# Another order for batch 0's attention and for batch 1's mixing in a fused sorted-attention and mixer kernel

## The chip, the cores and the metric

The kernel runs on one core of a Trainium2 chip. The metric is the device time of one execution in microseconds; unless a unit is given, numbers below are microseconds. The engines are TensorE (PE; its weight loads are listed as PEld), VectorE (DVE), ScalarE (ACT), GpSimd (POOL) and SyncE (SP). Here GpSimd issues all loads that change the type on the way, and SyncE issues the stores, the bounce through DRAM and the DMA transposes. Each engine takes its instructions strictly in order.

## The reference

Four batches, 8 heads, 768 rows of 64. The keys and values come in 8 blocks of 96 rows, and a small 8 x 8 matrix per head, normalized five times, mixes whole blocks. Attention is then block by block, and its output goes through a mixer with a token product and two channel products:

```python
for _ in range(5):
    P = P - np.max(P, axis=-1, keepdims=True)
    P = np.exp(P)
    P = P / (np.sum(P, axis=-1, keepdims=True) + 1e-09)
    P = P / (np.sum(P, axis=-2, keepdims=True) + 1e-09)
k_sorted = np.einsum('bhij,bhjcd->bhicd', P, k_b)
v_sorted = np.einsum('bhij,bhjcd->bhicd', P, v_b)
...   # softmax(q_b k_sorted^T / 8) v_sorted within each block, heads joined to x: 4 x 768 x 512
a1 = alpha1 * x + beta1
tok = np.einsum('ts,bsd->btd', w_tok, a1)
u = x + lam * tok
a2 = alpha2 * u + beta2
ch = np.maximum(a2 @ w_ch1, 0.0) @ w_ch2
return (u + lam * ch)
```

## The kernel before

**Stages.** Until about 12 the block matrix is normalized, on VectorE and ScalarE, while the first loads arrive. From 12 to 37 batch 0's attention runs. From then on the channel products of the mixer run, the largest part of the work, and the attention of the following batch is put in between them piece by piece. A batch has three groups g of 256 tokens. A group has eight steps `h` 0 to 7 (`h_unit`: eight matmuls with `W1p` into `h_ps`, then ReLU to `hT` on ScalarE) and then seven steps `c` (`ch_step`: products with `W2p` and with sums of it, in a scheme with seven half products, with `hs` as sums of `hT`); batch 0's group 0 has eight plain steps `c` instead (`ch_plain`).

**Where the order is set.** All of it is written out by hand. The table `at` holds, under a key (batch, group, h or c, step), what is issued right behind that step; `put` enters it and `run` issues it. What stands earlier in the program stands earlier in each engine's queue. An engine that waits holds up all that is queued behind it.

**Attention of batch 0.** `v_sort` copies columns of v into `VD` so that `v_mix` can mix the blocks on TensorE, 8 columns at a time, with a 512-wide filler matmul ahead; the result is copied to `Vs`. `k_turn` mixes and turns the keys of a pair of heads, and `k_copy` brings them to `KT0` in two parts. `score(b, g, hf)` computes scores for pair g and half hf of the blocks, and ScalarE takes the exponential into `et`. `pv_first` multiplies by `Vs` and VectorE divides by the sums into `x`. `permute` reorders the columns of `w_tok` into `wp`, `prep_wtok` transposes them. `first_mm`, `first_turn`, `first_finish` make the first group's channel input directly (`tok`, `z`, `a2T`); `first_back` makes its `u` and reads the row `brow`.

**Attention of the other batches.** `mix_v` (three pieces) mixes v on TensorE into `mixed`, `bounce_v` writes it to a DRAM scratch (`vscr`), `back_v` reads it back into `Vs` with the rows in the place wanted. `mix_k` (three pieces, four copies to `kT` each) makes the keys, `q_turn_late` or DMA transposes (`q_cross`) the queries. Then come eight scores and eight products `pv`, s0 to s7 and p0 to p7; p_n needs s_n's exponential and `Vs`. `half_done` (tails, `token_affine`) turns half of x into the token product's input `a`; `moe_tok` is the token product, `moe_cross` turns u by DMA transpose into `uT`, `moe_affine` scales it to `a2T`, which the steps `h` of its group read. `weights` prepares the sums of `W2p` on VectorE.

**Buffers and queues around the change.** There are two PSUM pools: `psA`, two buffers of two banks, used in turn by k_turn, scores, pv, mix_v and mix_k; and `psB`, four buffers of one bank. The third tile from a pool of two waits until the first has been read. `uT` and `brow`/`rrow` share two buffers, `raw` (the next batch's v and k) shares two with batch 0's k and v, and `wp` shares one with the first q. Each DMA that GpSimd issues carries one of eight semaphores in turn and waits for the DMA eight before it. GpSimd's queue is, in order: q, v, k, four loads of w_tok, alphaB, betaB, three v_sort copies, lamB, four loads of `W1p` (lines 179 and 180), `brow` (a product of betaB and lamB), four loads of `W2p` (line 317), `lift` (three operations on lamB, alphaB, betaB), then batch 1's v, k and q.

The lines that enter batch 1's work, as the kernel before has them:

```python
for n, at_ in enumerate((("h", 7), ("c", 0), ("c", 1))):
    put(0, 0, *at_, lambda n=n: mix_v(1, n, dve.tensor_copy))
put(0, 0, "c", 1, lambda: bounce_v(1))
put(0, 0, "c", 6, lambda: back_v(1))
seq = ("s0", "s1", "s2", "p0", "s3", "p1", "p2", "s4", "p3", "s5", "p4", "s6", "p5", "s7", "p6", "p7")
slots = [(1, "h", n) for n in range(1, 8)] + [(1, "c", n) for n in range(7)] + [(2, "h", n) for n in range(2)]
```

Of the kernel before, what the change touches and what calls it, by code (L numbers as in the profile page):

```python
# [16 lines left out]
def kernel(  # L17
# [156 lines left out]
    lamB = const([128, C], FT, "lamB")  # L174
    pool.dma_start(alphaB[:], moe_alpha1.partition_broadcast(128))
    pool.dma_start(betaB[:], moe_beta1.partition_broadcast(128))
    for lo, hi in ((8, 16), (16, 32), (32, 48)):
        v_sort(lo, hi, pool.tensor_copy)
    pool.dma_start(lamB[:], moe_lam.partition_broadcast(128))
    for g in range(4):  # L180
        pool.dma_start(W1p[:, :, g * 512:(g + 1) * 512], w1v[:, :, g * 512:(g + 1) * 512])
    brow = att.tile([128, C], F16, name="brow", tag="uT", bufs=2)
    rrow = att.tile([128, GS], F16, name="rrow", tag="uT", bufs=2)
    pool.tensor_tensor(brow[:], betaB[:], lamB[:], ALU.mult)

    vscr = dram.tile([B, H * NB, BLK, D], F16, name="vscr", tag="vscr")
# [50 lines left out]
    def turn_slab(src, rhs, g, name, ps):  # L237
        if ps is psa:
            ps = ps([128, 2, 512], FT, name)
            ps = [ps[:, a, 0:384] for a in range(2)]  # L240
        else:
            ps = [ps([128, 384], FT, name)[:] for a in range(2)]
        for s in range(12):
            for h2 in range(2):
                t = (s + 6 * h2) % 12
                r = slice(h2 * 64, h2 * 64 + 64)
                pe.matmul(
                    ps[t // 6][r, (t % 6) * 64:(t % 6) * 64 + 64],
                    src[r, g, t * D:(t + 1) * D], rhs(r, g), start=True, stop=True,
                )  # L250
        return ps
# [63 lines left out]

    for g in range(4):
        pool.dma_start(W2p[:, g * 4:(g + 1) * 4, :], w2v[:, g * 4:(g + 1) * 4, :])

    bigK = {}
# [68 lines left out]
    def k_copy(b, g, ps, half, eng):  # L388
        eng(
            KT0[:, g, :, :].rearrange("p i (th u) -> p (i th) u", th=2)[:, :, 0:HB].rearrange(  # L390
                "p x (c t) -> p x c t", t=12
            )[:, :, :, half * 6:half * 6 + 6],
            ps[half].rearrange("p (t x c) -> p x c t", t=6, c=4),
        )

# [464 lines left out]
    def wtok(ks, eng):  # L860
        prep_wtok(ks, 0, psb, eng)

    mix_values(0, psb)
    mix_keys(0, psb)
    warm(3)
    v_mix(0, 0, psb, act.copy)
    v_mix(0, 1, psb, act.copy)
    v_sort(48, 56, act.copy)
    v_mix(0, 2, psb, copy)
# [4 lines left out]
    v_mix(0, 3, psb, copy)  # L874
    v_sort(56, 64, act.copy)
    kp2 = k_turn(0, 2, psb)
    k_copy(0, 1, kp1, 0, copy)
    k_copy(0, 1, kp1, 1, act.copy)
    score(0, 0, 0, psa)
    kp3 = k_turn(0, 3, psb)  # L880
    k_copy(0, 2, kp2, 0, copy)
    k_copy(0, 2, kp2, 1, copy)
    score(0, 0, 1, psa)
    v_mix(0, 4, psb, copy)
    k_copy(0, 3, kp3, 0, copy)
    k_copy(0, 3, kp3, 1, copy)
    score(0, 1, 0, psa)
    v_mix(0, 5, psb, copy)
    score(0, 1, 1, psa)
    prep_scales()  # L890
    dve.tensor_copy(Vs[:, :, D:GRP], mgap[:].unsqueeze(2).to_broadcast([128, H * NB, GRP - D]))
    v_mix(0, 6, psb, copy)
    score(0, 2, 0, psa)
    v_mix(0, 7, psb, copy)
    score(0, 2, 1, psa)
    permute(0, copy, 0, 6)
    pv_first(0)
    score(0, 3, 0, psa)
    pv_first(1)
    for ks in range(3):  # L900
        wtok(ks, act.copy)
    score(0, 3, 1, psa)
    wtok(3, act.copy)
    wtok(4, copy)
    wtok(5, copy)
    permute(1, copy, 0, 6)
    first_mm(0, psb)
    row_sums(psb)
    pv_first(2)
    first_turn(0, psb)  # L910
    first_mm(1, psb)
    pv_first(3)
    first_turn(1, psb)
# [30 lines left out]
    put(0, 0, "c", 5, lambda: moe_affine(0, 1))  # L944
    put(0, 1, "h", 3, lambda: moe_affine(0, 2))
    for n, at_ in enumerate(((0, "c", 4), (0, "c", 6), (0, "c", 7), (1, "h", 0))):
        put(0, *at_, lambda n=n: weights(n))
# [10 lines left out]

    for n, at_ in enumerate((("h", 7), ("c", 0), ("c", 1))):
        put(0, 0, *at_, lambda n=n: mix_v(1, n, dve.tensor_copy))  # L960
    put(0, 0, "c", 1, lambda: bounce_v(1))
    put(0, 0, "c", 6, lambda: back_v(1))
    for n, at_ in enumerate((("c", 2), ("c", 4), ("c", 6))):
        put(0, 0, *at_, lambda n=n: mix_k(1, n, (act.copy,) * 4))
    for g, at_ in enumerate(((0, "c", 5), (0, "c", 6), (0, "c", 7), (1, "h", 0))):
        put(0, *at_, lambda g=g: q_turn_late(1, g, act.copy))
    put(0, 1, "h", 6, lambda: load_kv(2), lambda: load_q(2))
    seq = ("s0", "s1", "s2", "p0", "s3", "p1", "p2", "s4", "p3", "s5", "p4", "s6", "p5", "s7", "p6", "p7")
    slots = [(1, "h", n) for n in range(1, 8)] + [(1, "c", n) for n in range(7)] + [(2, "h", n) for n in range(2)]
    for what, at_ in zip(seq, slots):  # L970
        put(0, *at_, attn(1, what[0], int(what[1])))
    put(0, 1, "c", 3, half_done(1, 0))

    for b in range(1, B):
        p = b - 1
        if b > 1:
            for n, at_ in enumerate(((2, "h", 3), (2, "h", 5), (2, "h", 7)) if b == 2 else ((2, "h", 1), (2, "h", 3), (2, "h", 5))):
                put(p - 1, *at_, lambda b=b, n=n: mix_v(b, n, act.copy))
            put(p - 1, 2, "h", 7, lambda b=b: bounce_v(b))
            put(p - 1, 2, "c", 6, lambda b=b: back_v(b))  # L980
            for n in range(3):
                at_ = ((p - 1, 2, "c", 4), (p - 1, 2, "c", 6), (p, 0, "h", 1)) if b == 2 else (
                    (p - 1, 1, "c", 6), (p - 1, 2, "c", 4), (p - 1, 2, "c", 6)
                )
                put(*at_[n], lambda b=b, n=n: mix_k(b, n, (act.copy,) * 4))
            for kt in range(NT):
                put(p - 1, *((2, "h", 0) if b == 2 else (1, "c", 1)), lambda b=b, kt=kt: q_cross(b, kt))
            if b + 1 < B:
                put(p, 0, "c", 0, lambda b=b: load_kv(b + 1), lambda b=b: load_q(b + 1))
            for what, at_ in (  # L990
                ("s0", (0, "h", 5)), ("s2", (0, "c", 1)), ("p0", (0, "c", 3)), ("s4", (0, "c", 5)), ("p2", (1, "h", 1)),
                ("s6", (1, "h", 3)), ("p4", (1, "c", 1)), ("p6", (1, "c", 4)),
            ):
                for i in range(2):
                    put(p, *at_, attn(b, what[0], int(what[1]) + i))
            put(p, 1, "h", 2, half_done(b, 0))
        put(p, 2, "h", 2 if b == 1 else 0, half_done(b, 1))
        put(p, 2, "h", 6 if b == 1 else 5, lambda b=b: moe_tok(b, 0, psb))
        put(p, 2, "h", 7 if b == 1 else 6, lambda b=b: moe_tok(b, 1, psb), lambda b=b: moe_cross(b, 0))
        put(p, 2, "c", 5 if b == 1 else 4, lambda b=b: moe_affine(b, 0))  # L1000
        put(b, 0, "h", 0, lambda b=b: moe_tok(b, 2, psb))
# [59 lines left out]
```

The softmax here doesn't subtract the row's maximum and nothing guards it: scores larger than these inputs give would overflow.

## Time and profile before

| what | value |
|---|---|
| median of 10 runs (lowest to highest) | 270.19 (269.06 to 270.92) |
| the profiled execution | 269.38, span 267.5 |
| TensorE busy | 247.3, 92% |
| VectorE busy | 180.6, 67% |
| ScalarE busy | 157.2, 59% |
| GpSimd busy | 77.8, 29% |
| software DMA queue (GpSimd's loads) | 15.34 MB |
| TensorE's granted clock, mean | 0.995 of full speed |

How to read the profile: a row of a timeline has the start and the length in microseconds from the start of the span, the engine, the program's line (nearly all instructions are recorded by one helper, line 69, so groups are told apart by the tile names), the operation, out<-in with shapes, how many, and in brackets the idle time before it with what ended that. `SPq` and `ACTq` are DMA issues in those engines' queues. A row of a DMA view has the tensors, the issuing queue, how many, the size of each in KB as it lands and the median time from issue to landing. Matmul ends are modelled, and busy TensorE is not TensorE at its peak. An engine named as the releaser is the one that came last by the profile; where it had long been done, it was something else, often a DMA.

### The profile page before, as it was taken

Reading aid. Unit: us, or ns where it says so; the run is one execution under the profiler, and the core shown is the slowest. Engines: PE = TensorE matmul, PEld = TensorE weight load, DVE = VectorE, ACT = ScalarE, POOL = GpSimd, SP = SyncE. Lnnn points to the kernel's source line nnn. Section 1 sums busy time; section 2 is a strip of 40 time slices with the busy share of each in tenths; the row PEclk is TensorE's granted clock in tenths of the full one; section 3 lists DMA queues with packets and bytes.
Section 4 is the critical chain, followed back from the end, with each engine's and each line's share of the span. In section 5 each row is a group of like instructions: output and inputs, shape, how many; then the busy total and the mean of one; then the engine's idle time right before and its main releaser. Section 6 shows DMA issues by size and latency. Waiting matters only on the chain.

```text
span 267.5 us, 6547 instructions
## 1 busy us (share of the span) xinstructions
PE 247.3 (92%) x2665; PEld 189.1 (71%) x2665; DVE 180.6 (67%) x419; ACT 157.2 (59%) x278; POOL 77.8 (29%) x94
## 2 busy tenths in 40 slices
PE   8986999797899998999999999999997999999992
PEld 3464776455688666768898677678895787788881
DVE  5768667768478955346989855439899564555544
ACT  3676575169955747967655859685724435444440
POOL 8881962413820301109502103003003030030300
PEclk9999999999999999999999999999999999999998
DMA  5999999998999366799998243950202113220202
GB/s 102 201 209 188 206 206 215 193 176 189 162 216 94 100 99 157 136 102 160 159 191 89 78 98 110 155 75 15 66 2 78 39 38 82 43 64 18 69 20 70
DMA packets 68078, 31.25 MB, mean 117 GB/s; under 512 B 57216, under 2 KB 63888, under 8 KB 68048
## 3 DMA queue, kind: packets, MB, share of 16 engines
q0 software_dynamic: 26352, 15.34, 42.6%
q1 hardware_dynamic: 41504, 15.36, 32.4%
q8 instruction: 21, 0.34, 0.5%
q10 hardware_dynamic: 192, 0.13, 0.2%
q14 instruction: 9, 0.07, 0.1%
HBM read 32.78 MB, written 8.65 MB: 155 GB/s over the span
## 4 chain that ended last, share of the span: by engine, by line
PE 60%; DVE 18%; ACT 8%; DMA 6%; issue 4%; POOL 2%; ACTq 0%; DVEq 0%; SPq 0%; POOLq 0%
PE h_ps L69 20%; PE cha_ps L69 12%; PE tok_ps L69 10%; PE chb_ps L69 9%; DVE ost L69 4%; ACT kT L69 4%; DVE x L69 4%; DVE a L69 4%; DMA Vs<-vscr 3%; DMA v<-in_v_dram 3%; PE x_ps L69 3%; PE sc_ps L69 2%; DVE a2T L69 2%; PE v_ps L69 2%; DVE hs L69 1%
## 5 line engine op out<-in xcount | busy, mean ns | idle before, releaser
L69 PE MATMUL h_ps<-a2T,W1p 128*128 128x256 bf16 x768 | 93.2, 273 | 3.7 <-ACT qT L69 2.3
L69 PEld LDWEIGHTS <-W1p 128*128 128x128 bf16 x768 | 73.6, 98 | 17.0 <-issue 4.4
L69 POOL TENSOR_TENSOR ost<-ost,u 128x512 f32<-128x512 f32 x22 | 29.3, 1332 | 141.9 <-DVE ost L69 130.6
L69 ACT ACTIVATE hT<-h_ps 128x512 f16<-128x512 f32 x96 | 56.1, 601 | 24.4 <-PE h_ps L69 23.2
L69 PEld LDWEIGHTS <-hs 128*128 128x128 f16 x352 | 33.5, 98 | 5.5 <-issue 1.0
L69 PE MATMUL tok_ps<-a,w_tokT 128*128 128x512 f16 x132 | 32.1, 379 | 2.6 <-DVE a L69 2.0
L69 PEld LDWEIGHTS <-hT 128*128 128x128 f16 x296 | 28.3, 98 | 7.2 <-ACT hT L69 0.5
L69 DVE SCALAR_TENSOR_TENSOR u<-tok_ps,x 128x512 f32<-128x512 f32 x22 | 15.2, 691 | 26.9 <-PE tok_ps L69 26.6
L69 DVE TENSOR_TENSOR hs<-hT 128x512 f16<-128x512 f16 x44 | 18.5, 419 | 19.2 <-ACT hT L69 19.2
L69 ACT CAST u<-u 128x512 f16<-128x512 f32 x22 | 13.6, 617 | 29.4 <-DVE u L69 29.4
L69 ACT ACTIVATE et<-sc_ps 96x768 f16<-96x768 f32 (+1 forms) x32 | 25.0, 810 | 6.0 <-PE sc_ps L69 6.0
L69 ACT CAST kT<-kmix_ps 64x512 f16<-64x512 f32 x36 | 25.8, 718 | 3.1 <-PE kmix_ps L69 2.7
L69 ACT COPY ost<-cha_ps 128x256 f32<-128x256 f32 x33 | 12.3, 372 | 22.4 <-PE cha_ps L69 21.5
L69 PE MATMUL cha_ps<-T,hs 128*128 128x256 f16 x176 | 22.8, 272 | 0.7 <-ACT ost L69 0.7
L69 PEld LDWEIGHTS <-w_tokT 128*128 128x128 f16 x132 | 12.7, 98 | 15.0 <-DVE a L69 2.9
L69 PE MATMUL chb_ps<-W2p,hs 128*128 128x256 f16 x176 | 22.8, 273 | 0.0
L69 POOL DMA_DIRECT2D qn<-in_q_dram x18 | 15.9, 902 | 12.7 <-DMA W2p<-in_moe_w_ch_dram 7.2
L69 DVE TENSOR_TENSOR ost<-ost,lamB 128x256 f32<-128x256 f32 (+1 forms) x23 | 18.3, 795 | 0.4
L69 DVE TENSOR_TENSOR ost<-ost,chb_ps 128x256 f32<-128x256 f32 x22 | 9.2, 418 | 13.3 <-PE chb_ps L69 11.7
L69 DVE TENSOR_TENSOR x<-x_ps,rcb 96x512 f16<-96x512 f32 x24 | 16.5, 687 | 0.8
L69 PE MATMUL x_ps<-Vs,et 96*128 96x65 f16 (+4 forms) x288 | 12.8, 195 | 1.7 <-ACT et L69 0.9
L69 PEld LDWEIGHTS <-et 96*128 96x128 f16 (+4 forms) x288 | 12.0, 100 | 3.3 <-issue 1.4
(129 smaller groups left out, 315.1 us busy)
## 6 DMA issues: line engine op xcount, KB each, us to landing
out_dram<-ost SPq DMA_DIRECT2D x22, 192.0 KB, 2.2
raw<-in_v_dram POOLq DMA_DIRECT2D x6, 384.0 KB, 8.1
raw<-in_k_dram POOLq DMA_DIRECT2D x6, 384.0 KB, 12.0
qn<-in_q_dram POOLq DMA_DIRECT2D x18, 128.0 KB, 12.1
vscr<-mixed SPq DMA_DIRECT2D x6, 384.0 KB, 4.6
Vs<-vscr SPq DMA_DIRECT2D x3, 768.0 KB, 8.3
W1p<-in_moe_w_ch_dram POOLq DMA_DIRECT2D x4, 512.0 KB, 13.9
W2p<-in_moe_w_ch_dram POOLq DMA_DIRECT2D x4, 512.0 KB, 14.1
```

What stands on the lines that cost most here:

```text
L69: ins = getattr(self.eng, name)(*args, **kwargs)
```

## The change

Nothing that is computed is changed: the same matmuls, copies, loads and stores, with other engines, other parts and other places for some.

- Batch 0: v_sort for all columns from 8 on goes to GpSimd, in five copies ahead of betaB's load; the first permute of w_tok goes from VectorE (two copies) to GpSimd (four copies), behind the first `W1p` load; `brow` follows, and only then come the other three `W1p` loads and the four of `W2p`. k_copy's parts, for the pairs whose turn is in psA, are halves of the blocks and no longer halves of the rows within each block; for that turn_slab takes one region of 768 across the two banks. Scores come earlier, and pv_first, prep_wtok and the second permute later.
- Batch 1: mix_v, bounce and the weights' sums come one to three steps later, back_v one earlier; mix_k and q_turn_late alternate between ScalarE and VectorE; the scores and products take twelve steps in place of sixteen; half_done, moe_tok, moe_cross and moe_affine for its first group come earlier, and moe_affine(0, 2) later.
- Batches 2 and 3: mix_v of batch 2 two steps earlier; the third piece of mix_k on VectorE; half of batch 2's query transposes later; p6 one step earlier.

```diff
@@ before the attention of batch 0 (GpSimd)
     pool.dma_start(alphaB[:], moe_alpha1.partition_broadcast(128))
+    for lo, hi in ((8, 16), (16, 24), (24, 40), (40, 56), (56, 64)):
+        v_sort(lo, hi, pool.tensor_copy)
     pool.dma_start(betaB[:], moe_beta1.partition_broadcast(128))
-    for lo, hi in ((8, 16), (16, 32), (32, 48)):
-        v_sort(lo, hi, pool.tensor_copy)
     pool.dma_start(lamB[:], moe_lam.partition_broadcast(128))
-    for g in range(4):
+
+    def load_w1(g):
         pool.dma_start(W1p[:, :, g * 512:(g + 1) * 512], w1v[:, :, g * 512:(g + 1) * 512])
+
+    load_w1(0)
...
-    pool.tensor_tensor(brow[:], betaB[:], lamB[:], ALU.mult)
@@ turn_slab
-            ps = ps([128, 2, 512], FT, name)
-            ps = [ps[:, a, 0:384] for a in range(2)]
+            ps = ps([128, 16 * D], FT, name)[:, 0:12 * D]
+            ps = [ps[:, 0:384], ps[:, 384:768], ps]
@@ behind the normalization
-    for g in range(4):
-        pool.dma_start(W2p[:, g * 4:(g + 1) * 4, :], w2v[:, g * 4:(g + 1) * 4, :])
@@ k_copy
+        dst = KT0[:, g, :, :].rearrange("p i (th u) -> p (i th) u", th=2)[:, :, 0:HB]
+        if len(ps) == 3:
+            x = slice(8 * half, 8 * half + 8)
+            eng(
+                dst[:, x].rearrange("p x (c t) -> p x c t", t=12),
+                ps[2].rearrange("p (t x c) -> p x c t", t=12, c=4)[:, x],
+            )
+        else:
...
@@ batch 0
+    permute(0, pool.tensor_copy, 0, 3)
+    permute(0, pool.tensor_copy, 3, 6)
+    pool.tensor_tensor(brow[:], betaB[:], lamB[:], ALU.mult)
+    for g in range(1, 4):
+        load_w1(g)
+    for g in range(4):
+        pool.dma_start(W2p[:, g * 4:(g + 1) * 4, :], w2v[:, g * 4:(g + 1) * 4, :])
+
     mix_values(0, psb)
...
     score(0, 0, 0, psa)
-    kp3 = k_turn(0, 3, psb)
+    kp2 = k_turn(0, 2, psb)
+    score(0, 0, 1, psa)
...
-    permute(0, copy, 0, 6)
-    pv_first(0)
     score(0, 3, 0, psa)
-    pv_first(1)
-    for ks in range(3):
-        wtok(ks, act.copy)
+    wtok(0, copy)
+    wtok(1, copy)
     score(0, 3, 1, psa)
+    wtok(2, copy)
+    pv_first(0)
+    wtok(3, act.copy)
+    pv_first(1)
...
@@ batch 1
-    put(0, 1, "h", 3, lambda: moe_affine(0, 2))
-    for n, at_ in enumerate(((0, "c", 4), (0, "c", 6), (0, "c", 7), (1, "h", 0))):
+    put(0, 1, "c", 1, lambda: moe_affine(0, 2))
+    for n, at_ in enumerate(((0, "c", 7), (1, "h", 0), (1, "h", 1), (1, "h", 2))):
         put(0, *at_, lambda n=n: weights(n))
...
-    for n, at_ in enumerate((("h", 7), ("c", 0), ("c", 1))):
+    for n, at_ in enumerate((("c", 0), ("c", 1), ("c", 2))):
         put(0, 0, *at_, lambda n=n: mix_v(1, n, dve.tensor_copy))
-    put(0, 0, "c", 1, lambda: bounce_v(1))
-    put(0, 0, "c", 6, lambda: back_v(1))
-    for n, at_ in enumerate((("c", 2), ("c", 4), ("c", 6))):
-        put(0, 0, *at_, lambda n=n: mix_k(1, n, (act.copy,) * 4))
-    for g, at_ in enumerate(((0, "c", 5), (0, "c", 6), (0, "c", 7), (1, "h", 0))):
-        put(0, *at_, lambda g=g: q_turn_late(1, g, act.copy))
+    put(0, 0, "c", 2, lambda: bounce_v(1))
+    put(0, 0, "c", 5, lambda: back_v(1))
+    for n, at_ in enumerate((("c", 3), ("c", 4), ("c", 6))):
+        put(0, 0, *at_, lambda n=n: mix_k(1, n, (both[n % 2],) * 4))
+    for g, at_ in enumerate(((0, "c", 6), (0, "c", 7), (1, "h", 0), (1, "h", 1))):
+        put(0, *at_, lambda g=g: q_turn_late(1, g, both[1 - g % 2]))
...
-    for what, at_ in zip(seq, slots):
-        put(0, *at_, attn(1, what[0], int(what[1])))
-    put(0, 1, "c", 3, half_done(1, 0))
+    seq = (
+        "s0 s1", "s2", "p0 s3", "p1", "p2 s4", "p3",
+        "s5", "p4 s6", "p5", "s7", "p6", "p7",
+    )
+    for n, todo in enumerate(seq):
+        for what in todo.split():
+            put(0, 1, *(("h", 2 + n) if n < 6 else ("c", n - 6)), attn(1, what[0], int(what[1])))
+    put(0, 1, "c", 2, half_done(1, 0))
@@ batches 1 to 3
-            for n, at_ in enumerate(((2, "h", 3), (2, "h", 5), (2, "h", 7)) if b == 2 else ((2, "h", 1), (2, "h", 3), (2, "h", 5))):
+            for n, at_ in enumerate(((2, "h", 1), (2, "h", 3), (2, "h", 5))):
                 put(p - 1, *at_, lambda b=b, n=n: mix_v(b, n, act.copy))
...
-                put(*at_[n], lambda b=b, n=n: mix_k(b, n, (act.copy,) * 4))
+                put(*at_[n], lambda b=b, n=n: mix_k(b, n, (both[n == 2],) * 4))
...
-                put(p - 1, *((2, "h", 0) if b == 2 else (1, "c", 1)), lambda b=b, kt=kt: q_cross(b, kt))
+                at_ = (1, "c", 1) if b == 3 else (2, "h", 0) if kt < 3 else (2, "c", 0)
+                put(p - 1, *at_, lambda b=b, kt=kt: q_cross(b, kt))
...
-                    put(p, *at_, attn(b, what[0], int(what[1]) + i))
+                    put(p, at_[0], at_[1], at_[2] + (i if what == "p6" else 0), attn(b, what[0], int(what[1]) + i))
...
-        put(p, 2, "h", 2 if b == 1 else 0, half_done(b, 1))
-        put(p, 2, "h", 6 if b == 1 else 5, lambda b=b: moe_tok(b, 0, psb))
-        put(p, 2, "h", 7 if b == 1 else 6, lambda b=b: moe_tok(b, 1, psb), lambda b=b: moe_cross(b, 0))
-        put(p, 2, "c", 5 if b == 1 else 4, lambda b=b: moe_affine(b, 0))
+        put(p, *((1, "c", 6) if b == 1 else (2, "h", 0)), half_done(b, 1))
+        put(p, 2, "h", 5, lambda b=b: moe_tok(b, 0, psb))
+        put(p, 2, "h", 6, lambda b=b: moe_tok(b, 1, psb), lambda b=b: moe_cross(b, 0))
+        put(p, 2, "c", 4, lambda b=b: moe_affine(b, 0))
```

## The prediction

> **What bounds the kernel now.** I read the busy shares and the slices first, then TensorE's idle time, then GpSimd's timeline and the landings of its loads, last SyncE's queue. Numbers without a unit are microseconds.
>
> ```profile
> PE 247.3 (92%) x2665; PEld 189.1 (71%) x2665; DVE 180.6 (67%) x419; ACT 157.2 (59%) x278; POOL 77.8 (29%) x94
> ...
> GB/s 102 201 209 188 206 206 215 193 176 189 162 216 94 100 99 157 136 102 160 159 191 89 78 98 110 155 75 15 66 2 78 39 38 82 43 64 18 69 20 70
> ```
>
> TensorE is busy for 92% of the span, and neither kernel has a matmul more than the other. A reordering can therefore win only from the 20.2 in which TensorE idles, and 5.3 of that is the tail after 260, which stays as it is. The second line says that the loads run at about 206 GB/s from 5 to 50 without a pause. The idle places after batch 0's attention are these, in TensorE's timeline:
>
> ```profile
> 50.37 0.59 PE L69 MATMUL mix_ps<-raw,bigM 128*128 128x512 f16 x2 [1.88 <-DVE bigP L69]
> ...
> 67.60 1.03 PE L69 MATMUL h_ps<-a2T,W1p 128*128 128x256 bf16 x8 [2.25 <-ACT qT L69]
> 72.69 0.42 PE L69 MATMUL x_ps<-Vs,et 96*128 96x65 f16 x8 [0.30 <-DMA Vs<-vscr]
> ...
> 106.45 1.22 PE L69 MATMUL h_ps<-a2T,W1p 128*128 128x256 bf16 x7 [0.95 <-DVE a2T L69]
> ...
> 117.02 0.35 PE L69 MATMUL sc_ps<-qT,kT 64*128 64x96 f16 x8 [0.40 <-DVE sel L69]
> ...
> 167.44 1.46 PE L69 MATMUL tok_ps<-a,w_tokT 128*128 128x512 f16 x6 [0.46 <-ACT hT L69]
> ```
>
> The first row names VectorE, but bigP there is batch 2's and is not an input. What mix_v of batch 1 reads is raw, and the landings show it:
>
> ```profile
> raw<-in_v_dram POOLq DMA_DIRECT2D x1, 384.0 KB, 13.8
> ...
> raw<-in_v_dram POOLq DMA_DIRECT2D x2, 384.0 KB, 14.4
> ```
>
> The first half is issued at 34.59 and lands 13.8 later, at 48.4. The median over both halves is 14.4, so the second takes 15.0 from 35.15 and lands at 50.15. TensorE starts 0.2 later. So **the loads, not the work in front of them, set 50.37**, and whatever is saved before it is lost in this wait as long as batch 1's v lands then. GpSimd issues them:
>
> ```profile
> 16.61 0.54 POOL L69 DMA_DIRECT2D lamB<-in_moe_lam_dram  x1
> 17.14 2.38 POOL L69 DMA_DIRECT2D W1p<-in_moe_w_ch_dram  x3
> 21.80 0.74 POOL L69 DMA_DIRECT2D W1p<-in_moe_w_ch_dram  x1 [2.28 <-DMA wt<-in_moe_w_tok_dram]
> 26.40 1.16 POOL L69 TENSOR_TENSOR brow<-betaB,lamB 128x512 f16<-128x512 f16 x1 [3.87 <-DMA lamB<-in_moe_lam_dram]
> 27.51 3.17 POOL L69 DMA_DIRECT2D W2p<-in_moe_w_ch_dram  x4
> ```
>
> From the same view the four pieces of W1p land at 28.75, 31.1, 33.75 and 36.4, about 2.6 apart, the four of W2p at 38.9 to 46.8, then raw. One stream, and its order is the order of issue.
>
> The next limit is batch 1's sorted v, which goes out to DRAM and comes back (bounce_v, back_v):
>
> ```profile
> 64.05 0.52 SPq L69 DMA_DIRECT2D Vs<-vscr  x1
> ```
>
> It lands 8.5 later, at 72.56, and the first product with it (p0) starts at 72.69. Its issue stands in SyncE's queue behind the two out stores (59.56 to 61.33, released by GpSimd's ost at 59.54) and two transposes (61.44 to 63.95). So the 2.25 at 67.60 is not free to win either: it is 0.30 away from the next wait.
>
> **The change, part by part.**
>
> *Batch 0's attention (12 to 37).* ScalarE loses two vd copies (0.85 each). GpSimd does 5 in place of 3 (three of 0.86 and two of 1.52 make 5.6, against 3.9), but ahead of betaB's issue, from 12.2 instead of 12.92, so columns 16 to 23 are sorted at 13.9 and TensorE's third v_mix (15.25, held by POOL vd) moves up 0.55. Copying key turns by block halves lets score (0,0) start after one copy, and ScalarE's copy no longer follows VectorE's (a wait of 1.07 at 16.92). VectorE loses 0.62 of wp copies. With scores ahead of the products, the chain x, tok, z, a2T ends at about 34.3 by the durations of the rows instead of 36.95. I take 2.0 off for TensorE (bounds 0, if two key halves in one PSUM region hinder each other, and 2.6). It then reaches mix_v of batch 1, now after the first product step instead of before it, at 45.9 + 1.8 = 47.7. This is worth nothing if the load lands later than that, as it does by the next item; without that cover it would be 2.0.
>
> *GpSimd's queue.* alphaB, sort to 17.7, betaB and lamB to 18.8, W1p's first piece to 19.55. Then four wp copies, 1536 elements a partition: by the vd copies (768 in 1.52) 3.0, by the memset of vd (1024 in 1.01) 1.5; I take 3.0, being copies too, until 22.6. It ends before lamB lands (26.3 in the trace; its place in the stream is the same), so either end costs nothing. Then brow, 26.40 to 27.56 as now. Only then come three W1p issues (27.56 to 29.8), four of W2p (to 33.0), lift and its two products (3.8, to 36.9) and raw. W1p's second piece is thus issued 9.7 later, when the stream holds only the first piece, which lands at 28.75. **The stream runs dry.** A load into an empty queue is in the trace at the start: the first q, 384 KB issued at 1.24, takes 4.9, its twin lands 2.0 after it, so a restart costs 2.9. The second piece would land at 27.56 + 2.9 + 2.6 = 33.1 against 31.1, 2.0 later. The lower end is 0, if packets flow before the first piece is through (after raw's issue at 120.46 traffic picks up by 121.7, that is 1.2 on, or 28.8 here). I take **1.6**, nearer the q row because that queue was truly empty. All behind it moves by the same: W1p's third piece to 35.3, where TensorE needs it at 35.0; W2p to 40.5, before any use; raw.
>
> The Trainium skill, "DMA: Bandwidth & Descriptors" (Anatomy of one DMA), gives a fixed 2.0 for each DMA, most of it completion rather than setup, plus bytes over 436 GB/s. By it the piece (1 MB read) lands at 32.0 and the gap is 0.9, which would take 0.7 off my sum; the q row's 4.9 is longer than that rule, so I stay with the row.
>
> *Transposes beside the load.* uT waits for brow's buffer, whose last reader is first_back(1). Now it goes out at 52.14, after raw v; in the changed kernel first_back(1) runs at about 47.7, so it runs beside raw v. Under transposes raw k's second half needs 2.1 (52.1 to 54.2), against 1.75 for raw v's: 0.35 for each 384 KB. With some 1.5 such pieces I take **0.5** (0 to 1.0). mix_v of batch 1 then starts at 50.37 + 1.6 + 0.5 = 52.5.
>
> *From there to p0.* Now Vs is issued 13.7 after mix_v. In the changed order one product step (0.86) and first_back lie in front: c1, tok (1.29), mix, c2, mix, c3 with two more mixes of 0.43 end 5.2 on; VectorE's mixed copies (1.22 each) let ost end at 6.65, POOL 7.9, stores 9.7, transposes 12.3, Vs at 12.4. That is 1.3 less. Vs issues at 64.9, p0 starts at 64.9 + 8.6 = 73.5, **0.8 later** than 72.69. TensorE's own arrival there I get as 72.2: the qT wait is gone since VectorE takes four kT copies (2.9) and two of the four qT copies, and the 2.25 returns as a wait for Vs.
>
> *p0 to the end of batch 1's first product block.* Scores and products now take fewer steps, and moe_affine(0,2) (four a2T, 1.1) stands on VectorE right before p4's x. psA has two buffers, and p5 takes p4's. After p4 TensorE has s6 (0.27) and c2 (0.87); VectorE has ost 0.45, hs 0.75, a2T 1.1, then rcb and x 0.92, 3.2 in all, of which 1.35 lies beside them: a **new wait of 1.8** ahead of p5. VectorE gets to the second half of a about 0.3 after TensorE wants tok, now one hidden unit sooner. Against that go 0.20 (mix_v at 89.57), 0.44 (ost at 99.57) and 0.24 + 0.95 (a2T at 105 to 106, as tok, transposes and affine come a unit earlier and half of the qT transposes leave SyncE's queue in front of them). Sum **+0.3**; bounds -1.8, if VectorE keeps up, and +2.3.
>
> *Batches 2 and 3.* VectorE takes one of three kT sets of 2.9. ScalarE's hT comes sooner, and 0.40 + 0.17 at 117 and 0.46 at 167 go: **-1.0** (0 to -1.0). Splitting p6 and p7 alters nothing: the 1.65 at 206 follows from VectorE, dense from 194 to 206 in the same order.
>
> **Sum.** +0.8 + 0.3 - 1.0 = +0.1. The profiled execution took 269.38 (span 267.5); the median of ten runs is 270.19, 0.8 more. So 269.5 on the profile's scale and **270.3** on the median's, with its own range 269.4 to 271.3. A measurement tells about 0.2%, 0.54, from no change.
>
> **Rivals.**
> *The stream does not run dry* (gap and transposes 0): p0 is at 71.4, 1.3 earlier, then +0.3 and -1.0: **268.2**. For it speaks that packets take only 1.2 to appear; against it brow's row, which stands between.
> *VectorE becomes the bound from 75 to 95* (slower). In the trace tails take 1.86 instead of 0.89 and one ost 1.16 beside a GpSimd ost (201 to 203). If both tails and this ost meet it, x of p5 to p7 and a are late by about 2.0: **272.3**. It decides once VectorE loses more than 0.5, since no idle is left there. Against it: POOL's ost has other phases here.
> On this the Trainium skill, "SBUF — State Buffer" (the single rule), says that VectorE's two-port copies and GpSimd lock each other out for a whole instruction; the 1.86 agrees. By it each meeting costs up to one ost, 1.3, and the sum here would be 271.6 with one.
> *Batch 0's gain passes through* because raw was not the wait at 50.37: 2.0 earlier throughout and no dry stream: **266.5**.
> *The reordering does nothing* that its waits don't undo: 270.2.
>
> **How the numbers follow.** The sum as worked out 0.42, no dry stream 0.25, VectorE bound 0.25, gain passes 0.05, nothing 0.03. The first splits 0.08 faster, 0.20 same, 0.14 slower. Faster 0.08 + 0.25 + 0.05 = 0.38; same 0.20 + 0.03 = 0.23; slower 0.14 + 0.25 = 0.39. 268.0 to 272.3 reaches both larger rivals and leaves out the fast tail and what lies beyond them.
>
> **What would show it.** Right: GpSimd's second W1p issue near 27.5 and a dip in GB/s near 29; TensorE idle 4 to 5 before batch 1's first mix_ps, which starts near 52.5; Vs issued near 64.9 and x_ps waiting for it about 1; an idle of 1 to 2 between two x_ps behind VectorE's a2T near 82; no wait at 106, 117 and 167. Wrong: mix_ps at 50.5 or earlier, Vs before 64, no wait ahead of p5, or W1p landing late enough that h_ps waits for it.

## The result

The changed kernel takes 273.94 us (median of 15 runs, 271.31 to 280.19) against 270.28 for the kernel before (50 runs beside it). The ratio is 1.0109, with a 95% interval from 1.0087 to 1.0132: **slower by 2.9 us**. Ratios, here and below, leave out executions more than 1.5% above the fastest of the same kernel: five of these 15 (the other ten have a mean of 273.25, against 270.29 before), and none to four of each run below. The forecast was 270.3, with a range up to 272.3. Numbers without a unit are microseconds.

The profiled execution took 272.46 (span 270.7), 3.08 more than the one of before. The page of the changed kernel, busy shares and slices of GB/s:

```profile
PE 248.1 (92%) x2665; PEld 190.3 (70%) x2665; DVE 191.5 (71%) x432; ACT 145.5 (54%) x261; POOL 81.5 (30%) x100
...
GB/s 103 200 209 172 135 206 207 219 134 237 153 193 158 30 103 118 176 130 112 191 181 143 79 46 125 158 91 12 80 2 78 39 8 111 42 50 31 62 23 72
```

TensorE does the same work in nearly the same time (248.1 against 247.3), so most of the loss is idle time. The fourth and fifth slices, 172 and 135, are the hole in the load stream that the forecast speaks of. The chain of waits goes through it by name (start, length, what):

```profile
18.45 7.45 DMA lamB<-in_moe_lam_dram
26.04 1.16 POOL brow L69
27.20 2.25 POOL W1p L69 x3
29.45 2.96 POOL W2p L69 x4
...
36.81 13.89 DMA raw<-in_v_dram
52.82 13.98 DMA qn<-in_q_dram
```

One product on GpSimd, brow, waits for a 128x512 vector, lamB, and behind it in GpSimd's queue stand three pieces of W1p, then W2p, raw and q. From 25 to 30 the transfers fall to 83 GB/s; the same stretch of the kernel before, in the second fence, has 208 (last column, GB/s):

```profile
25.00:30.00 5.00, 4.24 (x93) 3.62 (x92) 3.66 (x11) 2.72 (x6) 3.96 (x5) 1.00 0.55 83
```

```profile
25.00:30.00 5.00, 3.53 (x71) 2.78 (x69) 3.30 (x7) 2.71 (x6) 3.60 (x5) 1.00 1.24 208
```

That leaves (208 - 83) GB/s x 5 us = 625 KB undone, 3.0 of the stream at 208 GB/s. In the kernel before the same product waits for lamB until 26.40, and W2p stands behind it too; there the pieces of W1p, issued ahead of it, fill the time. TensorE's idle time in the changed kernel, in its timeline:

```profile
36.28 0.27 PE L69 MATMUL h_ps<-a2T,W1p 128*128 128x256 bf16 x1 [2.17 <-DVE a2T L69]
...
52.67 0.59 PE L69 MATMUL mix_ps<-raw,bigM 128*128 128x512 f16 x2 [1.70 <-DMA raw<-in_v_dram]
...
66.84 0.29 PE L69 MATMUL qt_ps<-ident,qn 128*128 128x128 f16 x1 [2.46 <-DMA qn<-in_q_dram]
...
75.42 0.42 PE L69 MATMUL x_ps<-Vs,et 96*128 96x65 f16 x8
77.99 0.43 PE L69 MATMUL x_ps<-Vs,et 96*128 96x65 f16 x8 [0.52 <-DVE x L69]
...
86.30 0.35 PE L69 MATMUL sc_ps<-qT,kT 64*128 64x96 f16 x8 [0.23 <-DVE x L69]
...
98.16 1.47 PE L69 MATMUL tok_ps<-a,w_tokT 128*128 128x512 f16 x6 [2.17 <-DVE a L69]
```

mix_v of batch 1 starts at 52.67 instead of 50.37, the first product p0 at 75.42 instead of 72.69. No wait stands in front of p0 here: Vs had landed at 74.8 (66.63 + 8.2). The waits at 106 and 167 are gone and 0.17 of those at 117 is left; in their place stand 2.46 for the last q load and 2.17 for the second half of a. SyncE's queue from the sorted v's way out (vscr) to its way back (Vs):

```profile
58.44 1.15 SPq L69 DMA_DIRECT2D vscr<-mixed  x2
60.38 2.45 SPq L69 DMA_DIRECT2D out_dram<-ost  x2
62.94 2.89 SPq L69 DMA_TRANSPOSE uT<-u  x2
66.63 0.33 SPq L69 DMA_DIRECT2D Vs<-vscr  x1
```

Between the transposes' end (65.83) and Vs lie 0.8: the second transfer of vscr, issued at 59.0, lands 7.6 later, at 66.6, and Vs reads vscr.

### The profile page after: what moved, and what is told of

Its sections match the earlier page's. It is cut to its first block, busy times and chain, and to the rows that moved or that the text cites. A ratio compares the mean times of both kernels' runs of the same rounds, so it can differ in the third digit from the quotient of the medians.

```text
span 270.7 us, 6547 instructions
## 1 busy us (share of the span) xinstructions
PE 248.1 (92%) x2665; PEld 190.3 (70%) x2665; DVE 191.5 (71%) x432; ACT 145.5 (54%) x261; POOL 81.5 (30%) x100
## 4 chain that ended last, share of the span: by engine, by line
PE 53%; DVE 18%; DMA 16%; POOL 7%; issue 3%; ACT 1%; DVEq 0%; POOLq 0%; ACTq 0%
PE h_ps L69 18%; PE cha_ps L69 13%; PE chb_ps L69 10%; PE tok_ps L69 7%; DMA qn<-in_q_dram 5%; DMA raw<-in_v_dram 5%; DVE ost L69 5%; DVE x L69 3%; DMA v<-in_v_dram 3%; DVE a L69 3%; DMA lamB<-in_moe_lam_dram 3%; DVE kT L69 2%; POOL vd L69 2%; PE x_ps L69 2%; DVE T L69 2%
## 5 line engine op out<-in xcount | busy, mean ns | idle before, releaser
L69 DVE TENSOR_TENSOR ost<-ost,lamB 128x256 f32<-128x256 f32 (+1 forms) x23 | 19.2, 833 | 0.4
L69 ACT CAST kT<-kmix_ps 64x512 f16<-64x512 f32 x24 | 17.1, 715 | 3.0 <-PE kmix_ps L69 2.7
```

Source lines behind the costliest of these rows:

```text
L69: ins = getattr(self.eng, name)(*args, **kwargs)
```

## The experiments

Ratios are to the kernel before, run beside each. The theory, A at first: the hole in the load stream is the cause. The rival: loads only move an idle time about, and VectorE in front of tok decides.

### The two orders of GpSimd's queue in both kernels

```diff
 # in the changed kernel
-    pool.tensor_tensor(brow[:], betaB[:], lamB[:], ALU.mult)
     for g in range(1, 4):
         load_w1(g)
     for g in range(4):
         pool.dma_start(W2p[:, g * 4:(g + 1) * 4, :], ...)
+    pool.tensor_tensor(brow[:], betaB[:], lamB[:], ALU.mult)
```

> The changed kernel with GpSimd's product for brow moved behind the issues of W1p's pieces 2 to 4 and of W2p, so that these issue from about 21.6 on and no longer wait for lamB. Theory A (the dry stream and what follows from it is the cause): GB/s stay near 206 at 25 to 30, W1p lands at 28.7 to 36.4 as before the change, batch 1's raw v at about 50.3, mix_v near 51.0, the last key load of q near 61 to 62 so that no q_t transpose waits for it, the granted clock goes back to about 0.995, p0 starts near 72.6; time about 270.5, some 2.7 under the changed kernel. Rival B (the loads only shift an idle time; tok, mixed copies and VectorE decide the end): mix_v earlier by up to 2, p0 later than 74.5 all the same, time about 272.5 to 273.5.

```diff
 # in the kernel before
-    for g in range(4):
-        load_w1(g)
+    load_w1(0)
     brow, rrow = ...
     pool.tensor_tensor(brow[:], betaB[:], lamB[:], ALU.mult)
+    for g in range(1, 4):
+        load_w1(g)
```

> The kernel before with the one change that W1p's pieces 2 to 4 are issued behind GpSimd's product for brow, as in the changed kernel. Theory A: the stream dips at 25 to 30, W1p's second piece lands about 2 later (32.5 to 33), mix_v of batch 1 starts near 52.5 instead of 50.4 and the last q load lands beyond 63; time about 272.3, 2 over the kernel before. Rival B (absorbed by the idle time of 2.25 at 67.6, loads do not decide): mix_v near 52.5 but p0 within 0.5 of 72.7, time 270.3 to 270.7.

| time against the kernel before | W1p's pieces 2 to 4 ahead of brow | behind brow |
|---|---|---|
| the rest as before | 1 (270) | **1.0111** [1.0072, 1.0150] |
| the rest as changed | **1.0003** [0.9978, 1.0028] | **1.0109** [1.0087, 1.0132] |

Theory A holds in both directions: the order of one product and three load issues (in the changed kernel seven, since W2p's four move ahead of the product too) is worth 1.1%, and all that the change does besides is worth nothing that can be measured (0.1, within about 0.7). TensorE's timeline with brow late in the changed kernel:

```profile
50.54 0.59 PE L69 MATMUL mix_ps<-raw,bigM 128*128 128x512 f16 x2 [0.70 <-DMA raw<-in_v_dram]
...
64.39 0.23 PE L69 MATMUL qt_ps<-ident,qn 128*128 128x128 f16 x1 [2.15 <-DMA qn<-in_q_dram]
...
72.47 0.41 PE L69 MATMUL x_ps<-Vs,et 96*128 96x65 f16 x8 [0.66 <-DMA Vs<-vscr]
...
94.80 1.47 PE L69 MATMUL tok_ps<-a,w_tokT 128*128 128x512 f16 x6 [2.16 <-DVE a L69]
```

From 25 to 30 the stream moves 206 GB/s, and mix_v and p0 are back where they were before the change. The waits for q (2.15) and for a (2.16) stay, so they do not come from the hole. The one line of the expectation that failed is that the q wait would go. With brow early in the kernel before:

```profile
52.21 0.59 PE L69 MATMUL mix_ps<-raw,bigM 128*128 128x512 f16 x2 [3.56 <-DMA raw<-in_v_dram]
...
54.56 1.06 PE L69 MATMUL mix_ps<-raw,bigM 128*128 128x512 f16 x2
...
77.61 0.41 PE L69 MATMUL x_ps<-Vs,et 96*128 96x65 f16 x8 [1.68 <-DMA Vs<-vscr]
```

mix_v is 1.84 late, nearly as in the changed kernel, but p0 4.92 late. Two mix matmuls at 54.56 take 1.06 instead of 0.59, and the windows of this run have a granted clock of 0.50 from 54 to 56.

### The later schedule alone

The kernel before with only the tables of batches 1 to 3 (mix_v, mix_k, q, scores, products, tails, tok, weights, and who copies) of the changed one.

> The kernel before with only the changed schedule of batches 1 to 3 (where mix_v, mix_k, q transposes, scores, products, tails, token mixing and weights stand, and who copies kT and qT); batch 0's attention, GpSimd's queue and its loads as before. Theory A (the later schedule by itself is worth nothing: what it saves at 106, 117 and 167 it gives back in front of tok and at the q load): mix_v 50.4 to 50.6, a wait of about 2 for the last q load at 64, p0 at 72 to 73, a wait of about 2.2 for a in front of tok, time 269.8 to 270.6. Rival B (the forecast's terms without the dry stream: 0.5 for transposes, -1.3 to p0, +0.3, -1.0): 268.2 to 268.7.

1.0003 [0.9968, 1.0039]. The time is theory A's, and the forecast's terms without the hole fall, since by them 268.2 to 268.7 was due.

```profile
73.84 0.42 PE L69 MATMUL x_ps<-Vs,et 96*128 96x65 f16 x8 [3.81 <-DMA Vs<-vscr]
...
97.15 1.47 PE L69 MATMUL tok_ps<-a,w_tokT 128*128 128x512 f16 x6 [2.17 <-DVE a L69]
```

mix_v starts at 50.53 here, so p0 comes 23.3 behind it, against 22.3 in the kernel before. TensorE gets to p0 earlier, and finds no Vs. The wait of 2.17 for a is here with the new schedule alone. The expected q wait did not show in this execution.

### Two placements on TensorE

```diff
 # in the changed kernel; shortened
-    ... ((0, "c", 6), (0, "c", 7), (1, "h", 0), (1, "h", 1))      # q transposes of batch 1
+    ... ((1, "h", 0), (1, "h", 1), (1, "h", 2), (1, "h", 3))
```

> The changed kernel with batch 1's four q transposes on TensorE put two or three steps later, at the first four hidden units of its first group, so that TensorE does its keys and hidden products while the last q load is under way. Theory A (p0 is bound by the sorted v, which comes back near 75 whatever TensorE does): the wait of 2.46 for q falls below 0.8, p0 now waits for Vs and starts no earlier than 74.5; time 0.4 to 0.9 under the changed kernel, about 272.5, and up to 1 more if the clock no longer dips below 0.7 behind the gap. Rival B (the q wait is the only thing in front of p0): p0 near 73, time about 271.

1.0102 [1.0057, 1.0147], by two executions: no better. The profiled execution took 287.43, so only the order of events is read from it. The q wait is gone, and p0 waits for Vs instead, as theory A has it, but far longer:

```profile
81.86 0.62 PE L69 MATMUL x_ps<-Vs,et 96*128 96x65 f16 x8 [8.93 <-DMA Vs<-vscr]
```

Vs was issued at 66.17, as in the changed kernel, and took 15.6 instead of 8.2: with TensorE earlier, GpSimd's ost was earlier, and batch 2's raw loads went out at 68.19, 2.0 behind Vs (in the kernel before 2.65 behind it, in the one with brow late 4.9). That these loads slow Vs is argued from this one trace, not shown.

```diff
 # in the changed kernel; shortened
-        put(p, 2, "h", 5, moe_tok(b, 0))      put(p, 2, "h", 6, moe_tok(b, 1), moe_cross(b, 0))      put(p, 2, "c", 4, moe_affine(b, 0))
+        put(p, 2, "h", 6 if b == 1 else 5, ...)      "h", 7 if b == 1 else 6      "c", 5 if b == 1 else 4
```

> The changed kernel with batch 1's first token mixing (both halves, the cross product and the first affine) one hidden unit later, where the kernel before has it. Theory A (tok one unit too early costs, as VectorE has not brought a): the wait of 2.17 in front of tok falls to 1.3 or less and about 0.9 is won, time about 272.3. Rival B: the hidden units behind it then wait for a2T by about 1.2, as they did before the change, and the time stays within 0.4 of the changed kernel's.

1.0120 [1.0085, 1.0155]: rival B. The wait in front of tok falls as expected and comes back in front of the hidden units:

```profile
99.41 1.47 PE L69 MATMUL tok_ps<-a,w_tokT 128*128 128x512 f16 x6 [0.85 <-DVE a L69]
...
110.42 0.28 PE L69 MATMUL h_ps<-a2T,W1p 128*128 128x256 bf16 x1 [0.25 <-DVE a2T L69]
111.64 1.22 PE L69 MATMUL h_ps<-a2T,W1p 128*128 128x256 bf16 x7 [0.94 <-DVE a2T L69]
```

2.17 - 0.85 = 1.32 won, 0.25 + 0.94 = 1.19 returned. The kernel before has waits of 0.24 and 0.95 at the same two rows.

### VectorE's order in front of tok

```diff
 # in the changed kernel with brow late
-        put(p, *((1, "c", 6) if b == 1 else (2, "h", 0)), half_done(b, 1))
+        put(p, *((1, "c", 5) if b == 1 else (2, "h", 0)), half_done(b, 1))
```

> The changed kernel with brow's product behind the W1p and W2p issues (as tried) and, besides, batch 1's second half_done (tails and affine of a) one product step earlier, at c5, which puts these five VectorE instructions in front of three ost instructions (0.93 + 0.41 + 0.41 = 1.75). Theory A (VectorE's order alone sets the wait of 2.16 for a in front of tok): the wait falls to 0.2 to 0.6, time about 268.3 to 268.8, against 270.2 without. Rival B (the ost products then hold PSUM buffers or a2T, and the wait comes back within the next units): 270.0 to 270.5.

0.9998 [0.9973, 1.0023]. On the mechanism A, on the time B: tok starts without any wait, at 93.60 instead of 94.80, and two waits for hT appear behind it, one for an out store later:

```profile
99.67 0.28 PE L69 MATMUL cha_ps<-W2p,hT 128*128 128x256 f16 x1 [0.48 <-ACT hT L69]
...
100.67 0.28 PE L69 MATMUL cha_ps<-W2p,hT 128*128 128x256 f16 x1 [0.39 <-ACT hT L69]
...
140.79 1.03 PE L69 MATMUL cha_ps<-T,hs 128*128 128x256 f16 x8 [1.76 <-ACT ost L69]
```

Behind the waits for hT the gain is gone: the next product (cha_ps<-T,hs) starts at 101.46, against 101.58 with brow late alone. The 1.76 comes on top in this execution; ScalarE's copy before it had itself waited 2.97 for an out store to land. So VectorE's order does set the 2.16, and the 2.16 is still not free to win: ScalarE is the next limit, 6 behind tok.

### What makes 2.9 of a landing 2 late

Extra matmuls on zeros in mix_v's own PSUM buffer keep TensorE busy while it waits for raw (ten in the kernel before with brow early, eight in the changed one).

```diff
+        if (b, n) == (1, 0):
+            fill(ps[:, 0, :], 10)      # 8 in the changed kernel
         for m in range(2):
             pe.matmul(ps[:, m, :], bigM..., raw[...], start=True, stop=True)
```

> The kernel before with W1p's pieces 2 to 4 behind brow, as in the earlier trial, and ten matmuls of 128x512 on zeros (10 x 0.216 = 2.2 us at full clock) written into mix_v's own PSUM buffer in front of batch 1's first mix_v; they are extra work. Theory A (the wait of 3.56 for raw costs twice: its own length, and a granted clock of about a half for some 4 us behind it): no slice of the clock below 0.9 at 52 to 58, mix_v still near 52.2, p0 about 22.3 behind it at 74.6 instead of 77.6, time about 271.5 against 273.2 without the matmuls. Rival B (the slow stretch behind mix_v comes from the transfers, not from the clock): p0 at 77 or later, 273.0 to 273.5.

> The changed kernel with eight matmuls of 128x512 on zeros (1.7 us at full clock, extra work) in the PSUM buffer of batch 1's first mix_v, in front of it, so that TensorE is not idle for more than 1.5 there. Theory A (in most executions the wait for raw exceeds 2.4 and a slow clock behind it adds to the dry stream's 1.9): ratio to the kernel before 1.007 or less, 272 or less. Rival B (the landing alone costs the 2.9, by the collisions behind it): ratio 1.009 to 1.012, 272.7 to 273.5.

In the kernel before with brow early, the profile did what theory A says:

```profile
49.25 2.32 PE L69 MATMUL mix_ps<-wz 128*128 128x512 f16 x10 [0.78 <-DVE sel L69]
52.31 0.61 PE L69 MATMUL mix_ps<-raw,bigM 128*128 128x512 f16 x2 [0.73 <-DMA raw<-in_v_dram]
...
74.56 0.42 PE L69 MATMUL x_ps<-Vs,et 96*128 96x65 f16 x8 [0.23 <-DMA Vs<-vscr]
```

The clock is full behind the wait (1.00 from 50 to 58), p0 is 22.25 behind mix_v (25.4 without the matmuls), and the span is 269.4 instead of 272.4. But the runs say 1.0099 [1.0070, 1.0128] against 1.0111: no difference that can be told. In the changed kernel the eight matmuls give 1.0122 [1.0077, 1.0167], against theory A, and this trace:

```profile
65.94 0.23 PE L69 MATMUL qt_ps<-ident,qn 128*128 128x128 f16 x1 [1.19 <-DMA qn<-in_q_dram]
...
75.42 0.62 PE L69 MATMUL x_ps<-Vs,et 96*128 96x65 f16 x8 [2.05 <-DMA Vs<-vscr]
...
98.50 2.19 PE L69 MATMUL tok_ps<-a,w_tokT 128*128 128x512 f16 x6 [2.18 <-DVE a L69]
```

The q wait is halved and the clock is full to 74, yet p0 starts at 75.42, the very time of the changed kernel. Here Vs sets it: issued at 66.50, it landed 8.8 later. In the changed kernel Vs had landed at 74.8, so there the q wait and the slow clock behind it delayed p0 by at most 0.6; without them Vs would have. The clock then dips later (x_ps 0.62 instead of 0.42, tok 2.19 instead of 1.47).

The granted clocks on record bound what slow clocks can make up of the 2.9. Their means over the runs behind each ratio are 0.9866 for the changed kernel and 0.9909 with brow late, 0.9890 for the kernel before with brow early and 0.9921 for the kernel before beside it. Over some 270 these differences are 1.2 and 0.8 at most. With the ten matmuls the clock was no lower than that of the kernel before beside it (0.9895 against 0.9878), and the loss was still 1.0%. So most of the loss is the landing, 1.8 to 2.1 at mix_v, and what it meets behind it; the exact shares stay open.

### Raw v ahead of W2p's last pieces

If the landing of raw v is the limit, the same bytes in another order should win: after W2p's first piece, raw v, W2p's second, raw k, W2p's last two, then q.

```diff
+    load_w2(0)                       # in place of all four
 ...
             raw_of[(b, kv)] = raw
+            if b == 1:
+                for g in ((2, 3), (1,))[kv]:
+                    load_w2(g)
```

> The kernel before with batch 1's v load issued behind W2p's first piece, then W2p's second, the k load, W2p's last two and q: the same bytes in another order. Theory A (the landing of raw v sets mix_v, and with it the sorted v and p0): raw v lands near 43, mix_v starts at 48.5 without a wait for it, Vs is issued near 62.2, p0 starts near 70.9, time about 268.4. Rival B (the stream's end, the last q load near 61, or ScalarE's kT and qT copies set p0): p0 no earlier than 72.3, time 269.7 to 270.3.

> The changed kernel with brow's product behind W1p's issues and the same order of loads as in the other trial (W2p's first piece, raw v, W2p's second, raw k, W2p's last two, q). Theory A (loads alone): mix_v at 49.8 without a wait for raw instead of 50.5, p0 near 71.7, time about 269.4. Rival B (the last q load decides): TensorE arrives there 0.7 earlier and waits 2.8 instead of 2.15, the granted clock falls below 0.7 for 2 to 4 us behind the wait, p0 at 72.5 to 74, time 270.3 to 272.

In the kernel before: 0.9977 [0.9945, 1.0009], no difference that can be told. In this execution TensorE reached its first hidden products 0.86 later than in the profile of before, a difference that the edit does not explain, so mix_v starts at 50.14, without a wait for raw, and p0 at 72.69 as ever.

In the changed kernel with brow late: **0.9959 [0.9927, 0.9992]**, some 1.1 less than the kernel before and 4 less than the changed kernel. Over all of its twelve executions the gain is smaller (medians 269.76 and 270.31).

```profile
63.25 0.23 PE L69 MATMUL qt_ps<-ident,qn 128*128 128x128 f16 x1 [1.66 <-DMA qn<-in_q_dram]
...
72.23 0.42 PE L69 MATMUL x_ps<-Vs,et 96*128 96x65 f16 x8 [1.55 <-DMA Vs<-vscr]
```

mix_v starts at 49.88 with no wait, q comes earlier, and no slice of the clock is low. p0 wins only 0.24 over the kernel with brow late, as Vs is again what it waits for. This is the one version here whose interval lies below 1.

### Sorting batch 1's v two steps earlier

On top of that: mix_v at h6, h7 and c0 instead of c0, c1 and c2, bounce_v at c0. Three variants: Vs ahead of the out stores and the second transposes in SyncE's queue; with the q transposes a step later; and with half_done early as well.

```diff
 # shortened; this is the first of the three
-    ... (("c", 0), ("c", 1), ("c", 2))      bounce_v at "c", 2      back_v at "c", 5
+    ... (("h", 6), ("h", 7), ("c", 0))      bounce_v at "c", 0      back_v at "c", 1
```

> The changed kernel with brow late and raw v ahead of W2p's last pieces, as tried, and batch 1's three mix_v two steps earlier (h6, h7, c0), its way out to DRAM at c0 and its way back at c1, in front of the out stores and of the second pair of transposes in SyncE's queue. Theory A (the sorted v is what holds p0 there, by 1.55): Vs is issued near 60 instead of 63, p0 starts near 70.7 without a wait for it, time about 267.8, 1.3 under the kernel with raw first alone. Rival B (the transfers next to each other slow one another, and the q load comes later for it): q wait above 2.5, p0 at 72, time 269.3.

> As the last, with batch 1's four q transposes one step later each. Theory A (with Vs early the q load is the next limit): the q wait falls from some 1.7 to 0.8, p0 near 70, time about 267.2. Rival B (the keys' copies or VectorE hold p0): p0 within 0.3 of the kernel without this step, same time.

> As the last, with batch 1's second half_done one product step earlier. Theory A: the wait of 2.17 for a in front of tok goes and half of it stays won (as from 73 to 111 in the trial with brow late, 0.7 to 1.1), time about 266.3. Rival B (it comes back as a wait for out stores or hT): 267.2, as without it.

1.0021 [0.9990, 1.0052], 1.0013 [0.9981, 1.0045] and 1.0059 [1.0031, 1.0087]: no gain, and the third is slower than the kernel before. The first, TensorE and then VectorE:

```profile
70.13 0.41 PE L69 MATMUL x_ps<-Vs,et 96*128 96x65 f16 x8 [0.17 <-DMA Vs<-vscr]
...
83.03 0.35 PE L69 MATMUL sc_ps<-qT,kT 64*128 64x96 f16 x8 [2.81 <-DVE x L69]
```

```profile
81.03 1.12 DVE L69 TENSOR_SCALAR a2T<-uT,ab2col 128x256 bf16<-128x256 f16 x4 [2.50 <-DMA uT<-u]
```

p0 comes 2.1 earlier than with raw v first alone, as expected, and at 83 all of it is gone (the same score stood at 82.03 there): the transposes that now stand behind Vs go out at 67.88 instead of 60.42, VectorE's a2T waits for them, and x, which TensorE needs, is queued behind a2T.

> The kernel with raw v ahead of W2p's last pieces and mix_v two steps earlier, but with the way back of the sorted v between the out stores and the second pair of transposes in SyncE's queue (it stood ahead of both, and VectorE's a2T then waited 2.50 for the transposes at 81). Theory A (that wait alone ate the 2.1 won at p0): Vs is issued near 61.9, the transposes near 62.3, p0 starts near 70.5, no a2T wait above 0.5 at 81, the wait in front of tok back at 2.2; time about 268.0. Rival B (VectorE is full from 70 to 95, so that an earlier p0 is lost in front of tok whatever SyncE's order): p0 earlier than 71, tok no earlier than 93.5, time 269.2 or more.

> As the last, with batch 1's q transposes one step later. Theory A (the q wait of about 0.7 is all they can win): 267.7 to 268.0. Rival B (scores then wait for qT copies and et, as with the other order: 0.3 to 0.8 in three places): 268.0 to 269.

With Vs between the out stores and these transposes: 0.9974 [0.9942, 1.0006] and 0.9990 [0.9959, 1.0020], no difference that can be told. Neither theory is borne out whole. p0 is at 70.47 in the second, but the two transposes' issues, started at 62.72 beside Vs's own transfer, take 6.92 instead of 2.52, and a2T still waits 1.99. tok starts at 94.66, against 93.90 with raw v first alone: what was won at p0 is lost before 95.

## Why the prediction was wrong, step by step

- **"The stream runs dry"** was right in kind and nearly in size. GpSimd issued the three pieces at 27.14 (27.56 forecast); W1p's second and third piece landed at 32.6 and 35.9 (33.1 and 35.3). At "1.6" plus 0.5 for "Transposes beside the load" mix_v was to start at 52.5; it started at 52.67. That the sum fits so well is luck: with the stream put back and the transposes still beside the load, mix_v starts at 50.54, so the transposes cost 0.2 at most and the hole 2.1. The fixed 2.0 and 436 GB/s of the Trainium skill's "DMA: Bandwidth & Descriptors" (Anatomy of one DMA) would have the piece there 4.4 after its issue, an estimate from that page; 5.5 passed, as by the row of the first q.
- **"From there to p0"** is the step that failed first. Vs was to be issued 12.4 after mix_v, 1.3 less than before; it took 13.96. Of the 1.56 too few, 0.5 are the out stores (2.45 instead of 1.77, less what GpSimd's ost came earlier), 0.4 the transposes (2.89 instead of 2.51), and 0.7 a wait that I had not seen at all (a gap of 0.8 where I had 0.1): vscr has to land before Vs reads it. I counted SyncE's queue by durations of the quieter stretch of before, and moved it into the stretch where k, q, transposes and vscr run together. In six other runs with mix_v at c0 to c2 Vs came 13.0 to 13.5 after mix_v, against 13.7 before (and 15.8 with tok late, where the clock was slow behind mix_v), so of the 1.3 at most 0.2 to 0.7 was there. "The 2.25 returns as a wait for Vs" did not show in the changed kernel: there p0 has no wait, and a wait of 2.46 for the last q, landing at 66.8 instead of 60.6, stands in front. I had not looked at when q lands. With brow late or the later schedule alone the wait for Vs is there (0.66 and 3.81).
- **"p0 to the end of batch 1's first product block"**, +0.3: it was +1.0 (from p0 to the tok at 118.91; 115.17 before). "A new wait of 1.8" ahead of p5 was wrong: p5 did not wait at all. It starts at 84.78, before VectorE has read p4's product (85.33 to 86.25), so it did not take p4's buffer: the two buffers of psA are not taken strictly in turn. Waits of 0.52 and 0.23 came elsewhere. "0.3 late" for a was wrong by 1.9: the wait is 2.17. VectorE runs without a gap from 92 to 98 there. Its rows in the changed kernel and, in the second fence, in the kernel before:

```profile
84.30 1.11 DVE L69 TENSOR_SCALAR a2T<-uT,ab2col 128x256 bf16<-128x256 f16 x4
...
92.64 0.93 DVE L69 TENSOR_TENSOR ost<-ost,p 128x256 f32<-128x256 f32 x1
...
94.26 1.86 DVE L69 COPY x<-x 32x512 f16<-32x512 f16 x3
```

```profile
87.08 0.93 DVE L69 TENSOR_TENSOR ost<-ost,p 128x256 f32<-128x256 f32 x1
...
90.38 0.89 DVE L69 COPY x<-x 32x512 f16<-32x512 f16 x3
```

That is the rival **VectorE becomes the bound**, at its place. Its size (2.17, about 2.0 forecast) is partly luck: one of the two tails takes 1.86 instead of 0.89, beside a GpSimd ost, but the ost of 0.93 was as long before. From p0 to the end of a it is 2.1 more than before (22.69 against 20.57): 1.0 from that tail, 1.1 from the a2T of moe_affine(0, 2), which before came ahead of p0. Its time of 272.3 is not borne out: with the loads put back this wait is still there (2.16), and the kernel takes the time of before.

- **"Batches 2 and 3"**, -1.0: -0.5 by the same count (152.3 before, 151.8 after, from that tok to the end).
- **"Batch 0's attention"**, 2.0, "worth nothing" under the wait for raw: worth nothing was right, 2.0 was not. The hidden matmul that waits for a2T stands at 36.28 (35.15 with brow late; 35.22 before). ScalarE's key copies still wait for those on VectorE (1.29 at 17.42, 1.02 at 18.93), and that matmul waits 0.7 to 2.2 for a2T, which stands behind the second w_tok permutation on VectorE. So TensorE waits 1.70 for raw in front of mix_v, where 4 to 5 were forecast. The copies of wp on GpSimd took 1.86 and not 3.0; that cost nothing either way, as forecast, since brow waited for lamB until 26.04.
- **The sum.** Forecast +0.8, +0.3, -1.0; the trace has +2.73, +1.0, -0.5, which is the 3.2 by which the span grew. Put by cause: the hole costs 2.9 where I gave it 2.1 through its landing (transposes included), and the other terms, -2.0 in all (-1.3, +0.3, -1.0), are 0 within about 1 by two runs (brow late, the later schedule alone). Most of the error is gains that I had credited from single rows of a trace whose next waits I did not price.
- **"The stream does not run dry"**, 268.2: with the stream put back the kernel takes the time of before, so this rival had its price wrong too. (The 266.5 of the rival **Batch 0's gain passes through** is 266.2 by its own terms, 268.2 less 2.0.)

## What to carry to other kernels

Before an instruction is put in front of DMA issues in a queue, ask what it waits for: here one product of 1.2 us on a 128x512 vector held back seven loads of 512 KB, and its place alone makes the whole of the loss. That loads stand behind a wait is no harm while enough bytes are queued ahead of it, as three pieces of W1p were in the kernel before. When a chain is moved in time, its transfers get new neighbours; take their durations from a stretch that is as crowded as the new one, and name for each load, the last of the queue too, when it is first needed. An idle time that is removed is worth only what the next engine in line can give: the runs with tok late, half_done early and mix_v early each won 1.2 to 2.1 at one place and lost it again within some 15 us.

## What the runs showed of the hardware

**Waits of little over 2 can halve TensorE's clock.** Granted clocks behind each wait, in windows of 2 us, or the duration of six tok matmuls, which take 1.47 at full clock:

| TensorE's wait | behind it |
|---|---|
| 2.25 (before), 2.15 (brow late) | 1.00 |
| 2.46 for q (changed) | 0.54 and 0.61 for 4 us |
| 2.09 for q (half_done early) | 0.58 and 0.57 for 4 us |
| 2.05 for Vs (changed, extra matmuls) | 0.80, 0.50, 0.84 |
| 2.17 for a (changed) | tok takes 1.47 |
| 2.18 for a (changed, extra matmuls) | 0.78 and 0.50; tok takes 2.19 |
| 2.95 for raw (q late) | 1.00 |
| 3.33 for raw (tok late) | 0.66, 0.50, 0.50, 0.63 |
| 3.56 for raw (brow early) | 0.82, 0.50, 0.83 |
| 3.81 for Vs (later schedule alone) | 0.68, 0.50, 0.97 |
| 8.93 for Vs (q late) | 0.50 by the wait's end |

Between 2.05 and 2.95 both happen; every wait of 3.3 and more that I looked at behind 40 was followed by a slow clock. What decides between the two is not shown. The Trainium skill, "TensorE: Matmul & The Clock Gate" (Part 1, the HAM clock gate), has a free-running window of about 3.4 us and bids one avoid gaps above that; the half clock agrees, but here gaps of 2.05 to 2.46 were enough, so by these runs 3.4 is no safe length.

**A stream that runs dry need not stop.** From 25 to 30 it moved 83 GB/s and not 0, since the first piece of W1p, landing at 28.4, was still in it. By bytes the hole is 3.0 of the stream; mix_v, behind it, started 2.1 later than with brow late (52.67 against 50.54).

**Issues slow down with the traffic they join.** Two transposes took SyncE 2.5 in front of Vs's transfer and 6.9 beside it; Vs took 8.2 to 10.0 to land in eleven profiled executions, and 15.6 in the one with q late.
